# Attention of the second pair one step earlier, and both high casts ahead of the subtractions, in a fused attention and expert kernel

## The chip, the cores and the metric

The kernel runs on one core of a Trainium2 chip. The metric is the device time in microseconds (us) of one execution; three runs of the kernel before gave 1276.99, 1277.06 and 1277.22 us, median 1277.06. The profile is of one further execution.

## The reference

```python
def sm_attn(qq, kk, vv):                     # softmax(scale * qq kk^T) vv
    s = scale * np.matmul(qq, kk.transpose(0, 1, 3, 2))
    s = s - np.max(s, axis=-1, keepdims=True)
    a = np.exp(s)
    a = a / (np.sum(a, axis=-1, keepdims=True) + 1e-09)
    return np.matmul(a, vv)
p_packed = sm_attn(p, k, v)                  # 8 batches, 8 heads, 32 x 64
x = sm_attn(q, p_packed, p_packed)           # 8, 8, 576 x 64 -> 4608 x 512
for e in range(4):                           # p = domain_probs / its row sum
    h = np.maximum(x @ w1[e], 0.0)           # 512 x 1024
    out += p[:, e:e + 1] * (h @ w2[e])       # 1024 x 512
```

All is float32.

## The kernel before, in words

TensorE's share is written as 64 units. A unit is one batch `b` (576 tokens) and one chunk `ch` of 512 hidden columns (8 chunks: 4 experts, two halves each). Batches go in four pairs `sb`; within a pair the order is chunk by chunk, first the pair's even batch, then its odd one. Units are called u0 to u63 here, so from u3 on an even number is an even batch; u0 to u15 belong to the first pair, u16 to u31 to the second. The kernel's `step` is `2 * ch + b % 2`, which is the unit's number within its pair (only u1 and u2 are exchanged).

A unit does three things on TensorE, interleaved by hand. Seven products (`product`, index `i` from 0 to 6, 12 matmuls each, a scheme of seven products for a two by two block product) multiply this unit's hidden block with w2. Four groups (`mm1_groups`, 12 matmuls each) make the next unit's hidden block. And every even unit from u4 on forms the folded rows of the next chunk for both batches (`g_form`): packed values times w1, so that the second attention product and w1 become one matmul. `g_form` is a generator; the loop advances it after product 3 and after product 6, one row `g` each time, or in most units of the later pairs both rows in one advance (`rows = [range(NG)]`).

Every operand of the large matmuls is kept as a high and a low half. ScalarE casts the high half (`hi_of`, line 119), and the low half is a subtraction (`lo_of`, line 123), on VectorE for folded rows (`ghl`), on GpSimd for the products' operands (`st`), for the w2 operands (`tt`) and for the attention weights (`xl`). One PSUM tile `dbl` of two banks holds one row `g` of both batches, a bank each. There are four such tiles, which fill PSUM, so a matmul whose tile is still being read waits, and so does all of TensorE behind it.

Lines that the steps below touch: 71 and 81 (matmuls, by one helper or another), 76 (transposes), 391 (VectorE evicts a hidden block), 734 (VectorE sums of hidden blocks), 781 (sums of w2 blocks), 863 (VectorE adds a product to its sum), 896 (the seven sums combined after a batch's last chunk).

Attention of a later pair runs inside the units of the pair before it, as four generators: `pack_unit` for g = 0 and 1 (packed values of four heads each: load k, load v, scores, exponentials, transposes, product with v), then `tok_unit` for g = 0 and 1 (token weights: load q, scores, VectorE transposes into tile `a` at line 269, maximum at 274, exponentials on ScalarE at 279, sum at 289, division at 295, transpose at 304, high and low halves). For the first pair `AT_FIRST` names the steps at which each generator is made; at that moment what is left of the one before is drained. A generator is advanced once after every second product, and after every product from the third piece's step on. Each piece serves both batches of the pair.

The order of instructions on an engine is not the order of the text. A planner places them by their readiness in its own model of time, with the text's order as priority; only TensorE's groups and a few marked instructions are tied by hand. So on VectorE, ScalarE, GpSimd and on the queue of SyncE the order is fixed before the run, and an instruction that waits holds up all behind it on its engine. The program waits by tile.

Of the kernel before, what the change touches and what calls it, by code (L numbers as in the profile page):

```python
# [42 lines left out]
def attention_moe(ctx: ExitStack, tc: tile.TileContext, q, k, v, p, dp, w1, w2, out):  # L43
    nc = tc.nc
# [33 lines left out]
    def together(calls):  # L78

        for i, kw in enumerate(calls):  # L80
            ins = nc.tensor.matmul(**kw).ins  # L81
            for prev in order["free"] if i == 0 else []:
                after(ins, prev)
            if order["last"] is not None:
                after(ins, order["last"])
            order["last"] = ins
        order["free"] = []

    def dbl():
        return banks["dbl"].tile([P, 2, 512], F32, name="dbl")  # L90
# [21 lines left out]
    def cols(b, hh):  # L112

        i = (hh + b) % 2
        return slice(i * NPK, (i + 1) * NPK)

    def hi_of(dst, src, eng):
        if eng is nc.scalar:
            return nc.scalar.copy(out=dst, in_=src)  # L119
        return eng.tensor_copy(out=dst, in_=src)  # L120

    def lo_of(dst, src, hi, eng):
        return eng.tensor_tensor(out=dst, in0=src, in1=hi.bitcast(F32), op=ALU.subtract)  # L123
# [187 lines left out]
    def w1_load(ch, prs=range(NPAIR)):  # L311
        e, hf = divmod(ch, F // FC)
        res = []
        for pr in prs:
            raw = wpool.tile([P, FC], F32, name="wraw", bufs=4)
            load = nc.sync.dma_start(out=raw, in_=w1[e, pr * P:(pr + 1) * P, hf * FC:(hf + 1) * FC])
            res.append(raw)
        marks.setdefault(("w1", ch), load.ins)
        return res
# [3 lines left out]
    def g_tile(kept=False):  # L323
        if kept:
            return glast.tile([P, 2, FC], F32R, name="ghl6")
        return gpool.tile([P, 2, FC], F32R, name="ghl", bufs=5)

    def g_form(bs, ch, raws, rows=None, kept=None):

        for gr in rows or [[g] for g in range(NG)]:  # L330
            pss, calls = {}, []
            for g in gr:
                ps = dbl()
                pss.update({(b, g): ps[:, b % 2] for b in bs})
                for hs in range(4):
                    pr, hh = 2 * g + hs // 2, hs % 2
                    part = slice(hh * D, (hh + 1) * D)
                    for b in bs:
                        c0 = (hs // 2) * 2 * NPK + cols(b, hh).start
                        calls.append(dict(  # L340
                            out=pss[b, g][c0:c0 + NPK, :], lhsT=ppbd[b % 4][part, pr, cols(b, hh)],
                            rhs=raws[pr][part, :], start=True, stop=True,
                        ))
            together(calls)
            tiles = {(b, g): g_tile((b - bs[0], g) == kept) for b in bs for g in gr}
            for g in gr:
                for b in bs:
                    ghl = tiles[b, g]
                    hi_of(ghl[:, 0, :], pss[b, g], nc.scalar)
                    marks[b, ch, g, "low"] = lo_of(ghl[:, 1, :], pss[b, g], ghl[:, 0, :], nc.vector).ins  # L350
                    gs.setdefault((b, ch), []).append(ghl)
            yield
# [8 lines left out]
    def load_probs(b, e):  # L361
        t = wpool.tile([P, S], F32, name="pbt", bufs=2)
        nc.sync.dma_start(out=t, in_=pnd[e:e + 1, b * S:(b + 1) * S].partition_broadcast(P))
        pbt[b] = t
# [60 lines left out]
    def first_loads(pools):  # L425

        b = units[0][2]
        nfull = S // P
        r = S - nfull * P
        pt = small.tile([P, NPAIR, NPK], F32, name="pt")  # L430
        nc.sync.dma_start(out=pt, in_=p[b])
        kts, vts = [], []
        for g in range(NG):
            kts.append(pools[g].tile([P, 2, S], F32, name="kt"))
            nc.sync.dma_start(out=kts[g], in_=k[b][:, 2 * g:2 * g + 2, :])
        for g in range(NG):
            vt, vr = pools[g].tile([P, nfull, 4 * D], F32, name="vt"), pools[g].tile([P, 4 * D], F32, name="vr")
            nc.sync.dma_start(
                out=vt, in_=v[b, 0:nfull * P, g * 4 * D:(g + 1) * 4 * D].rearrange("(c p) d -> p c d", p=P),
            )  # L440
            nc.sync.dma_start(out=vr[0:r], in_=v[b, nfull * P:S, g * 4 * D:(g + 1) * 4 * D])
            vts.append([vt[:, c, :] for c in range(nfull)] + [vr])
        xs[b] = x_tiles(b)
        qts, raws = [], []
        for g in range(NG):
            qts.append(att_tile(b, [P, 2, S], "kt"))
            nc.sync.dma_start(out=qts[g], in_=q[b][:, 2 * g:2 * g + 2, :])
            raws += w1_load(0, range(2 * g, 2 * g + 2))
        return pt, kts, vts, qts, raws
# [473 lines left out]
    def drain(gen):  # L923
        for _ in gen:
            pass
# [6 lines left out]
    with ExitStack() as first:  # L932
# [9 lines left out]
        pt, kts, vts, qts, raws = first_loads(pools)  # L942
# [28 lines left out]
    GROUPS = {1: ((0, 0),), 3: ((0, 1),), 4: ((1, 1),), 6: ((1, 0),)}  # L971
    GROUPS_LAST = {1: ((0, 0),), 3: ((1, 0),), 4: ((0, 1),), 6: ((1, 1),)}
    GROUPS_LATE = {4: ((0, 0), (0, 1)), 5: ((1, 1),), 6: ((1, 0),)}
    AT_FIRST = ((4, pack_unit, 0), (7, pack_unit, 1), (9, tok_unit, 0), (12, tok_unit, 1))
    def second_tile(n):
        beside = {}

        def new(b, shape, name):
            if name == "kt" or name == "vt" and n == 1:
                return xpool.tile(shape, F32, name=("xh2", "xl2", "xh3", "xh2")[n] if name == "kt" else "xl3")  # L980
            if name == "vr":
                beside["at"] = att_tile(b, [P, 4 * D + len(SC) * P], "kt")
                return beside["at"][:, 0:4 * D]
            if name == "at" and n == 1:
                return beside["at"][:, 4 * D:].rearrange("p (c s) -> p c s", s=P)
            return att_tile(b, shape, name)
        return new
# [13 lines left out]
    for u, (sb, ch, b) in enumerate(units):  # L1001
# [4 lines left out]
        if sb + 1 < SB:  # L1006
            pair = [2 * sb + 2, 2 * sb + 3]
            for at_step, make, g in AT_FIRST if sb == 0 else AT_LATER:
                if at_step == step:
# [5 lines left out]
        if u == 2 or u == 3:  # L1015
            gsteps = g_form([1] if u == 2 else [0, 1], u - 1, raws)
            drain(gsteps)
            raws = w1_load(u)
        elif 3 < u <= AHEAD and not odd and nsb < SB:
            how = {}  # L1020
            if sb > 0:
                turn = ch if u < AHEAD else NCH - 2
                how["kept"] = (1, 0) if turn == 0 else (None, (0, 1), (1, 1))[(turn - 1) % 3]
                if turn > 0:
                    how["rows"] = [range(NG)]
            gsteps = g_form([2 * nsb, 2 * nsb + 1], nch, raws, **how)
# [20 lines left out]
        for i in range(NPROD):  # L1047
# [27 lines left out]
            if u == 1 and i == 3:  # L1075
                drain(second)
                drain(g_form([1], 0, raws))
                raws = w1_load(1)
            for _ in range(SECOND[u][i] if u in SECOND and i < len(SECOND[u]) else 0):
                next(second, None)  # L1080
            if i == 4 and u > 1 and u + 2 < len(units) and units[u + 2][1] % 2 == 0:
                load_probs(units[u + 2][2], units[u + 2][1] // 2)
            if i in (EVEN if odd or sb == 0 else AROUND) or sb == 0 and step >= AT_FIRST[2][0]:
                next(back, None)
# [16 lines left out]
        if u == 0:  # L1101
            raws = w1_load(0)
            load_probs(1, 0)
        elif not odd and u > 2:
            nsb, nch = (sb, ch + 2) if ch + 2 < NCH else (sb + 1, ch + 2 - NCH)
            if nsb < SB:
                raws = w1_load(nch)
# [34 lines left out]
```

## Time and profile before

| | |
|---|---|
| median of three runs | 1277.06 us |
| profiled execution | 1276.54 us |
| its span, first to last instruction | 1274.8 us |
| busy in the span: TensorE, VectorE, GpSimd, ScalarE | 1257.8, 962.5, 852.7, 494.4 us |
| TensorE's granted clock | 1.00 of full speed |

Engines are PE (TensorE), PEld (its weight loads), DVE (VectorE), ACT (ScalarE), POOL (GpSimd) and SP (SyncE, which issues nearly all DMAs). A line like "A <- B: t, n, m" in a view of waits says that A stood idle t us in all, n times, at most m us, until B had finished. Stretches of one unit are cut at the first matmul of the unit's first product, found by counting 84 product matmuls to a unit.

### The profile page before, as it was taken

To read this page: it belongs to the slowest core of one execution; us is meant where nothing else is said; L and a number is where in the kernel's file an instruction comes from. 1 tells how busy PE (TensorE), PEld (TensorE's weight loads), DVE (VectorE), ACT (ScalarE), POOL (GpSimd) and SP (SyncE) were. 2 spreads that over 40 slices of the span, in tenths; PEclk is the share of its full clock that TensorE was granted. 3 is DMA by queue.
4 is the path that set the end of the run, shared out by engine and by line. 5 is a ranking of instruction groups with operands and counts; after the bars stand their busy time and mean duration, and the time that the engine had idled before them with its cause. 6 is when DMAs were issued, how large, how long until landed. Compare 5 with 4: busy or idle time off the path is not lost.

```text
span 1274.8 us, 26918 instructions
## 1 busy us (share of the span) xinstructions
PE 1257.8 (99%) x10784; PEld 1172.9 (92%) x10784; DVE 962.5 (76%) x1315; ACT 494.4 (39%) x893; POOL 852.7 (67%) x564
## 2 busy tenths in 40 slices
PE   9999999999999999999999999999999999999998
PEld 6889998998999999999999999999999999999998
DVE  6866767899975767997786667799679567766776
ACT  4644545646344333333335423333323533333321
POOL 3779887898995545666578454476568755556575
PEclk9999999999999999999999999999999999999999
DMA  9995556635455554454454546433536443444562
GB/s 327 352 327 195 193 186 209 206 117 188 161 204 198 177 168 142 158 169 152 149 158 160 173 159 200 154 120 114 158 126 214 153 136 115 129 154 131 176 218 99
DMA packets 91708, 223.94 MB, mean 176 GB/s; under 512 B 9280, under 2 KB 32192, under 8 KB 91584
## 3 DMA queue, kind: packets, MB, share of 16 engines
q1 hardware_dynamic: 90768, 221.92, 52.6%
q8 instruction: 86, 1.41, 0.5%
q10 hardware_dynamic: 816, 0.30, 0.1%
q14 instruction: 38, 0.31, 0.1%
HBM read 183.31 MB, written 38.87 MB: 174 GB/s over the span
## 4 chain that ended last, share of the span: by engine, by line
PE 68%; POOL 15%; DVE 10%; issue 3%; ACT 2%; DMA 1%; SPq 0%; ACTq 0%; DVEq 0%; POOLq 0%
PE dbl L71 63%; POOL st L123 9%; PE dbl L81 4%; DVE sblk L734 3%; POOL tt L123 2%; POOL acc L896 2%; DVE ghl L123 1%; DVE acc L863 1%; DVE ablk L391 1%; POOL xl L123 1%; POOL b L781 1%; PE bank L81 1%; PE dbl L76 1%; ACT ghl L119 1%; ACT st L119 1%
## 5 line engine op out<-in xcount | busy, mean ns | idle before, releaser
L71 PE MATMUL dbl<-st,tt 128*128 128x288 f32 x5376 | 763.5, 296 | 6.3 <-POOL st L123 1.9
L71 PEld LDWEIGHTS dbl<-st,tt 128*128 128x128 f32 x5376 | 721.5, 188 | 50.4 <-issue 25.2
L123 POOL TENSOR_TENSOR st<-sblk,st 128x576 fp32r<-128x576 f32 x248 | 390.5, 1583 | 232.1 <-ACT st L119 219.6
L71 PE MATMUL dbl<-xh,ghl 128*128 128x288 f32 x2016 | 406.5, 294 | 2.2 <-DVE ghl L123 2.2
L123 POOL TENSOR_TENSOR st<-ablk,st 128x576 fp32r<-128x576 f32 x191 | 289.9, 1522 | 136.6 <-ACT st L119 130.0
L863 DVE TENSOR_TENSOR acc<-dbl,acc 128x576 f32<-128x576 f32 x385 | 287.7, 751 | 101.4 <-PE dbl L71 99.9
L71 PEld LDWEIGHTS dbl<-xh,ghl 128*128 128x128 f32 x2016 | 321.8, 188 | 2.9 <-DVE ghl L123 2.9
L391 DVE SCALAR_TENSOR_TENSOR ablk<-dbl,pbt 128x576 f32<-128x576 f32 x252 | 189.4, 752 | 140.9 <-PE dbl L71 140.2
L71 PE MATMUL dbl<-xl,ghl 128*128 128x288 f32 x1008 | 295.8, 294 | 0.0
L119 ACT CAST st<-sblk 128x576 fp32r<-128x576 f32 x252 | 170.7, 677 | 279.8 <-DVE sblk L734 221.2
L119 ACT CAST st<-ablk 128x576 fp32r<-128x576 f32 x193 | 130.6, 677 | 251.5 <-PE dbl L71 226.4
L71 PEld LDWEIGHTS dbl<-xl,ghl 128*128 128x128 f32 x1008 | 188.9, 188 | 0.3 <-POOL xl L123 0.3
L734 DVE TENSOR_TENSOR sblk<-ablk 128x576 f32<-128x576 f32 x126 | 136.5, 1084 | 9.2
L119 ACT CAST ghl<-dbl 128x512 fp32r<-128x512 f32 x124 | 70.7, 588 | 112.5 <-DVE ghl L123 58.1
L123 DVE TENSOR_TENSOR ghl<-dbl,ghl 128x512 fp32r<-128x512 f32 x124 | 83.4, 687 | 20.1 <-ACT ghl L119 18.0
L734 DVE TENSOR_TENSOR sblk<-ablk,sblk 128x576 f32<-128x576 f32 x63 | 78.0, 1238 | 5.4
L81 PE MATMUL dbl<-wraw,ppbd 64*32 64x512 f32 x992 | 64.5, 597 | 0.4 <-DVE acc L863 0.4
L123 POOL TENSOR_TENSOR tt<-b,tt 128x512 fp32r<-128x512 f32 x42 | 61.7, 1480 | 3.3 <-ACT tt L119 3.2
L734 DVE TENSOR_TENSOR sblk<-sblk,ablk 128x576 f32<-128x576 f32 x63 | 57.7, 915 | 1.2
L896 POOL TENSOR_TENSOR acc<-acc,acc 128x576 f32<-128x576 f32 x28 | 43.5, 1562 | 12.5 <-DVE acc L863 12.5
L861 ACT COPY acc<-dbl 128x576 f32<-128x576 f32 x55 | 35.3, 642 | 37.1 <-PE dbl L71 37.1
L896 DVE TENSOR_TENSOR acc<-acc,acc 128x576 f32<-128x576 f32 x28 | 33.3, 1195 | 0.6
(137 smaller groups left out, 475.9 us busy)
## 6 DMA issues: line engine op xcount, KB each, us to landing
tt<-td SPq DMA_DIRECT2D x192, 512.0 KB, 4.3
wraw<-in_w SPq DMA_DIRECT2D x136, 256.0 KB, 3.7
td<-tt SPq DMA_DIRECT2D x56, 512.0 KB, 3.7
pbt<-pnd SPq DMA_DIRECT2D x32, 288.0 KB, 4.1
out<-acc SPq DMA_DIRECT2D x31, 288.0 KB, 2.4
kt<-in_k SPq DMA_DIRECT2D x14, 576.0 KB, 6.2
kt<-in_q SPq DMA_DIRECT2D x14, 576.0 KB, 5.6
vt<-in_v SPq DMA_DIRECT2D x15, 512.0 KB, 5.7
```

The lines of the kernel that those rows point to most:

```text
L71: res = nc.tensor.matmul(**kw)
L76: on_pe(nc.tensor.transpose(**kw))
L81: ins = nc.tensor.matmul(**kw).ins
L119: return nc.scalar.copy(out=dst, in_=src)
L123: return eng.tensor_tensor(out=dst, in0=src, in1=hi.bitcast(F32), op=ALU.subtract)
L391: res = nc.vector.scalar_tensor_tensor(out=a, in0=ps[:, :, 0:HS], scalar=0.0, in1=probs.rearrange("p (o t) -> p o t", o=1).broadcast_to([P ...
L734: marks["sum", u, name] = nc.vector.tensor_tensor(out=t, in0=blk(x), in1=blk(y), op=op).ins
L781: op = eng[m].tensor_tensor(out=blk[place], in0=blk[x], in1=blk[y], op=ALU.subtract).ins
L861: marks["evicted"] = nc.scalar.copy(out=dst, in_=src).ins
L863: res = nc.vector.tensor_tensor(out=accs[b, i], in0=ps, in1=accs[b, i], op=ALU.add)
L896: eng.tensor_tensor(out=m[dst], in0=m[x], in1=m[y], op=op)
```

## The change

`g_form` gets a switch `apart`. With it, ScalarE's high casts of all tiles of one advance are written first, and then VectorE's subtractions; without it, cast and subtraction of a tile stand together, tile after tile. It is on in every even unit from u4 on that forms folded rows, but for u16 (`ch` is the chunk of the unit in which the rows are formed, so `ch > 0 or sb > 1` leaves out only the second pair's first unit). The four attention pieces for the second pair are made at steps 3, 6, 8 and 11 in place of 4, 7, 9 and 12. The rule that a generator is advanced after every product follows the third piece, so it holds from step 8 on.

```diff
-    def g_form(bs, ch, raws, rows=None, kept=None):
+    def g_form(bs, ch, raws, rows=None, kept=None, apart=False):
...
             tiles = {(b, g): g_tile((b - bs[0], g) == kept) for b in bs for g in gr}
+            for g in gr if apart else ():
+                for b in bs:
+                    hi_of(tiles[b, g][:, 0, :], pss[b, g], nc.scalar)
             for g in gr:
                 for b in bs:
                     ghl = tiles[b, g]
-                    hi_of(ghl[:, 0, :], pss[b, g], nc.scalar)
+                    if not apart:
+                        hi_of(ghl[:, 0, :], pss[b, g], nc.scalar)
                     marks[b, ch, g, "low"] = lo_of(ghl[:, 1, :], pss[b, g], ghl[:, 0, :], nc.vector).ins
...
-    AT_FIRST = ((4, pack_unit, 0), (7, pack_unit, 1), (9, tok_unit, 0), (12, tok_unit, 1))
+    AT_FIRST = ((3, pack_unit, 0), (6, pack_unit, 1), (8, tok_unit, 0), (11, tok_unit, 1))
...
         elif 3 < u <= AHEAD and not odd and nsb < SB:
             how = {}
+            how["apart"] = ch > 0 or sb > 1
```

## Rows read from the trace of the kernel before

**Rows 1.** The page: busy time, share of the span and instructions of each engine.
```profile
PE 1257.8 (99%) x10784; PEld 1172.9 (92%) x10784; DVE 962.5 (76%) x1315; ACT 494.4 (39%) x893; POOL 852.7 (67%) x564
```
**Rows 2.** Windows, three stretches: length, then busy us (count) of each engine.
```profile
102.98:362.44 259.46, 254.47 (x2228) 236.16 (x2221) 218.49 (x272) 125.94 (x281) 230.62 (x152) 1.00 0.54 188
362.44:672.18 309.74, 308.43 (x2682) 289.70 (x2681) 234.76 (x329) 111.12 (x183) 191.29 (x125) 1.00 0.50 162
1030.90:1067.73 36.83, 36.83 (x297) 35.28 (x297) 25.83 (x35) 11.63 (x18) 20.72 (x14) 1.00 0.43 137
```
**Rows 3.** Waits of TensorE, from u3 to the end of u8.
```profile
PE dbl L76 <- ACT ppn L233: 0.9, 2, 0.5
PE dbl L76 <- ACT a L198: 0.8, 1, 0.8
```
**Rows 4.** Waits of TensorE, from u9 to the end of u16.
```profile
PE dbl L71 <- DVE ghl L123: 1.8, 1, 1.8
PE dbl L71 <- POOL st L123: 0.6, 2, 0.4
PE dbl L71 <- DVE acc L863: 0.6, 1, 0.6
```
**Rows 5.** Waits of TensorE, from u17 to the end of u32.
```profile
PE dbl L71 <- DVE ghl L123: 0.9, 2, 0.5
```
**Rows 6.** Windows of u8 to u14: as Rows 2.
```profile
203.64:226.56 22.92, 22.48 (x255) 19.86 (x252) 14.77 (x20) 10.19 (x23) 16.16 (x12) 1.00 0.53 172
226.56:245.33 18.77, 18.77 (x165) 17.96 (x166) 16.38 (x25) 13.97 (x48) 15.11 (x11) 1.00 0.61 207
245.33:265.04 19.71, 19.71 (x167) 17.71 (x165) 19.54 (x25) 9.89 (x21) 19.71 (x13) 1.00 0.58 203
265.04:283.32 18.28, 17.71 (x140) 17.50 (x133) 16.26 (x19) 7.07 (x12) 17.56 (x13) 1.00 0.39 132
283.32:304.43 21.11, 21.11 (x198) 18.26 (x196) 19.75 (x28) 16.20 (x53) 17.55 (x13) 1.00 0.65 231
304.43:324.41 19.98, 18.06 (x140) 17.59 (x133) 18.80 (x22) 7.39 (x13) 19.38 (x13) 1.00 0.26 97
324.41:344.54 20.13, 19.78 (x166) 17.71 (x164) 19.83 (x23) 7.96 (x13) 20.13 (x13) 1.00 0.54 183
```
**Rows 7.** Windows of u9, u10, u12 and u13, instructions on tile a alone.
```profile
226.56:245.33 18.77, 0.00 (x0) 0.00 (x0) 3.81 (x7) 6.93 (x31) 0.00 (x0) 1.00 0.61 207
245.33:265.04 19.71, 0.00 (x0) 0.00 (x0) 5.09 (x5) 1.18 (x5) 0.00 (x0) 1.00 0.58 203
283.32:304.43 21.11, 0.00 (x0) 0.00 (x0) 5.21 (x9) 8.24 (x36) 0.00 (x0) 1.00 0.65 231
304.43:324.41 19.98, 0.00 (x0) 0.00 (x0) 3.33 (x3) 0.00 (x0) 0.00 (x0) 1.00 0.26 97
```
**Rows 8.** Timeline of u13's start, VectorE and ScalarE: start, duration, instruction, idle before.
```profile
308.11 1.83 DVE L295 TENSOR_TENSOR a<-a,s 128x576 f32<-128x576 f32 x1
309.86 0.68 DVE L123 TENSOR_TENSOR ghl<-dbl,ghl 128x512 fp32r<-128x512 f32 x1
...
310.57 0.59 ACT L119 CAST ghl<-dbl 128x512 fp32r<-128x512 f32 x1 [3.05 <-DVE ghl L123]
```
**Rows 9.** All instructions of line 295: duration ns least, median, most.
```profile
L295 DVE TENSOR_TENSOR a<-a,s x13: 760/1514/1990, 65.9 to 875.3; 128x576 f32<-128x576 f32 x13
```
**Rows 10.** Waits of all engines: ScalarE's high casts behind VectorE.
```profile
ACT ghl L119 <- DVE ghl L123: 58.1, 57, 3.2
```
**Rows 11.** Timeline in u24: casts, subtractions and the stall.
```profile
534.48 0.58 ACT L119 CAST ghl<-dbl 128x512 fp32r<-128x512 f32 x1
...
535.82 1.07 ACT L119 CAST ghl<-dbl 128x512 fp32r<-128x512 f32 x2 [0.76 <-DVE ghl L123]
...
536.44 1.29 DVE L123 TENSOR_TENSOR ghl<-dbl,ghl 128x512 fp32r<-128x512 f32 x2 [0.65 <-ACT ghl L119]
...
537.39 3.40 PE L71 MATMUL dbl<-st,tt 128*128 128x288 f32 x24 [0.46 <-DVE ghl L123]
```

## The prediction

> **What bounds the kernel now.** First the page's busy times, to see which engine fills the span: TensorE is busy 1257.8 of 1274.8 us [rows 1]. The granted clock is 1.00, so the matmuls can't run faster, and the change takes none away. What it can win is TensorE's idle time alone. Second, windows by stage show where that lies. Two units without attention take 36.83 us with no idle time; u3 to u15 have 259.46 - 254.47 = 4.99 us of it, u16 to u31 only 309.74 - 308.43 = 1.31 [rows 2]. (The end of a matmul is modelled, so a stall is some 0.1 to 0.2 us longer than its row; I leave that out.) Third, the waits of TensorE name who is late. From u3 to u8 it is the packing piece on ScalarE: 0.9 us for two transposes of the packed values and 0.8 for one after the exponentials [rows 3]. From u9 to u16 it is VectorE and GpSimd: 1.8 us for the low half of a folded row, 0.6 for a product's sum on VectorE (a PSUM tile not yet free), 0.6 for low halves of the products on GpSimd [rows 4]. From u17 on it is the folded rows again, 0.9 us in two stalls [rows 5], and the same answer comes for the next sixteen units.
>
> Why VectorE is late shows in the windows by unit: it is busy 19.54 of 19.71 us in u10, 19.75 of 21.11 in u12, 18.80 of 19.98 in u13, 19.83 of 20.13 in u14; u8 has 14.77 of 22.92 [rows 6]. The token pieces' work on VectorE is 3.81 + 5.09 = 8.90 us for the one in u9 and u10 and 5.21 + 3.33 = 8.54 for the one in u12 and u13 [rows 7]. The largest stall, at the start of u13, ends with a subtraction of a folded row that stood behind the token division, 1.83 us long [rows 8].
>
> **The change part by part.**
>
> *Packing pieces (steps 4 and 7 to 3 and 6).* Loads, scores, exponentials, casts and products are the same in number. What changes is the kind of unit: the first began in an even unit and now begins in an odd one, the second the other way round. The late exponentials belong to the odd start (u7), a transpose of packed values was late at the last advance of either piece [rows 3]. So I expect the same 0.9 + 0.8 us at other places: 0. Ends: the 0.8 goes, or comes twice, so -0.8 to +0.8. The loads of k and v go to SyncE's queue a unit earlier; a load takes effect by the tile that it waits for, and that tile comes free a unit earlier too. No wait of TensorE on a load stands in rows 3 to 5: 0.
>
> *Token pieces (steps 9 and 12 to 8 and 11).* Nothing is added; VectorE's 8.90 and 8.54 us move, and GpSimd's low halves with them. I take each piece's split by the kind of unit in which it starts: 5.21 + 3.33 from an even start, 3.81 + 5.09 from an odd one. Taken out of rows 6, VectorE without tokens needs 14.77 (u8), 16.38 - 3.81 = 12.57 (u9), 19.54 - 5.09 = 14.45 (u10), 16.26 (u11), 19.75 - 5.21 = 14.54 (u12), 18.80 - 3.33 = 15.47 (u13), 19.83 (u14). Put in again one unit earlier: u8 19.98 of 22.92, u9 15.90 of 18.77, u10 14.45 of 19.71, u11 20.07 of 18.28, u12 19.63 of 21.11, u13 15.47 of 19.98. So u8 takes 5.21 us where there was room for 8.15, and u13 and u14, which follow one another with no room, get 3.33 us back. The sore place becomes u11: 1.79 us over. Part of its 16.26 is work left from u10, whose own excess goes, and the scores' matmuls lengthen u11 too, so I expect a stall of about the size of today's at u11, 0.6, and 0.4 for GpSimd's share. Of 1.8 + 0.6 + 0.6 = 3.0 us [rows 4], 1.0 stay: -2.0. Ends: all 3.0 go; or u11's excess adds 1.8 to what is there. Between them I am nearer to the first, because the excess is worked out for one unit and the room in u8, u9 and u10 together is 2.94 + 2.87 + 5.26 = 11.1 us.
>
> *High casts first.* A folded row's tile holds both batches, and the second batch's cast waits today until the first batch's subtraction has ended: ScalarE stands idle 58.1 us in 57 such waits [rows 10]. None of that is TensorE's time except where the row is late. In u24 the order is cast at 534.48, subtraction, casts from 535.82, subtractions from 536.44 to 537.73, and a product waits until 537.39 for the row's PSUM tile [rows 11]. Now both casts of the row end by about 534.48 + 1.07 = 535.55. The subtraction then waits for the second cast, as today the cast waits for the subtraction. Two subtractions take 1.29 us [rows 11] and end at 536.84. The first row's second one ends today 0.64 after 536.44, at 537.08: 0.24 earlier. Four such stalls, two in each of the two answers of 0.9 [rows 5], give -1.0. Ends: all four go, -1.8; or four new ones of that size appear where VectorE now waits for the second cast with sums and evictions behind it, +1.8. Some twenty further advances of the later pairs have no stall (rows 5 names all), so each has slack today, and a wait of one cast is 0.58 [rows 11]; that is why I stay near the row.
>
> In the first pair the same edit ends ScalarE's wait of 3.05 us at 310.57 [rows 8], behind which casts for the products stood. That helps GpSimd's lateness, and I count it in the 2.0.
>
> What the row doesn't show is whether the subtraction has to wait for the second cast at all. The Trainium skill, "PSUM — Partial Sum Buffer", section "Specifications (TRN2)", says that ScalarE and VectorE can read PSUM in parallel as long as no bank collides; the two batches lie in different banks. By that rule the first subtraction could run beside the second cast. Rows 10 and 11 speak against it for this program, which waits by tile; by the rule the part would be -1.8 and not -1.0.
>
> Sum: 0 - 2.0 - 1.0 = -3.0 us. The profiled execution took 1276.54 us (span 1274.8 and 1.7 around it), so 1273.5 by its own time; it lies 0.5 below the median of the runs, and from the median 1277.06 - 3.0 = **1274.1 us**.
>
> **Rivals.**
>
> *The stall only moves.* VectorE's work is the same in sum, and u3 to u15 use 218.49 of 259.46 us of it [rows 2]; what was late at u11 and u13 is then late at u9 and u12. For it: u12's even start was followed by the worst stall, and the even start is now u8's. Against it: u8 has room. Then only the casts pay: 1277.06 - 1.0 = 1276.1.
>
> *Slower: the division in front of the folded rows, twice.* Line 295 takes 0.76 us at best and 1.99 at worst [rows 9], at the tail of each token piece. If the planner puts it in front of the subtraction at u9 as it did at u13, the 1.8 comes there. At u11 the 1.79 over delays the rows for u12, and since u12 is then full (19.63 + 1.79 = 21.42 of 21.11) the delay lasts into u13, another 1.8. With today's 0.6 of GpSimd that is 6.0 for 3.0; if the casts give nothing the time is 1280.1. It decides itself at u11: with less than about 1 us over, u12 catches up. Speaking for this case is the Trainium skill, "SBUF — State Buffer", section "SBUF: two separate sides": VectorE with two SBUF inputs and GpSimd exclude one another for a whole instruction. Row 9's spread agrees with it, and GpSimd is busy 17.56 of 18.28 us in u11 [rows 6].
>
> *Nothing holds the subtraction back.* By bank, the four late stalls go and the sum is -3.8: 1273.3. The skill's PSUM rule, above, would have it so; rows 10 and 11 don't.
>
> *The casts' order doesn't change much.* The planner decides by its own times, and ScalarE's order may come out as before, since it doesn't see the stall. Then 1277.06 - 2.0 = 1275.1.
>
> **How the numbers follow.** A measurement of this kernel can tell 0.2% from no change, 2.55 us: faster means below 1274.5, slower above 1279.6. My forecast has 0.42: 0.36 of it below 1274.5, since its terms add up to anything from -4.6 to -1.5, and 0.06 within. The stall that moves has 0.29 (0.27 within, 0.02 slower). The division twice has 0.12, all of it slower. No hold by bank has 0.09, all faster. The order unchanged has 0.08 (0.06 within, 0.02 faster). Faster 0.47, same 0.39, slower 0.14. The range reaches down to 1271.5 (all of rows 4 and most of the late stalls) and up to 1278.5; the forecast alone has 1272.5 to 1275.6.
>
> **What would show it.** Right: windows of u8 with VectorE near 20 us and of u13 well under 18; no wait of 1.8 us on a folded row at u13; two casts of a row back to back on ScalarE and its waits behind VectorE nearly gone; the four late stalls at 0.2 each. Wrong: a wait on a folded row at u9 or u12 as long as the old one, or u14 and u15 as full as before, or stalls on the transposes of the packing pieces that add up to more than 1.7. The prediction fails as a whole if TensorE's idle time from u3 to u15 stays at 5.

## The result, and the profile after

The change makes the kernel slower by 0.7%: 1286.99 us, the median of four runs (1284.06 to 1287.93), against 1277.03 (1276.92 to 1277.22, four runs). The ratio is 1.0072, with a 95% interval of 1.0059 to 1.0084. Forecast was 1274.1, in a range of 1271.5 to 1278.5.

The profiled execution after took 1287.34 us, 10.8 more than the 1276.54 of before. The page first, with the busy times.

```profile
PE 1261.1 (98%) x10784; PEld 1176.6 (92%) x10784; DVE 949.6 (74%) x1315; ACT 491.3 (38%) x893; POOL 851.0 (66%) x564
```

The instructions are as many as in [rows 1], but TensorE is busy 3.3 us longer with them. The windows of u3 to u15 and of u16 to u31 (length, busy us and count of each engine, granted clock, DMA share, GB/s) say where the time went:

```profile
103.88:374.82 270.94, 258.79 (x2229) 239.91 (x2221) 221.89 (x273) 126.05 (x282) 229.84 (x152) 0.98 0.53 181
374.82:682.76 307.94, 307.57 (x2682) 289.61 (x2681) 229.22 (x328) 109.43 (x181) 188.82 (x125) 1.00 0.50 162
```

Against [rows 2], u3 to u15 take 270.94 - 259.46 = 11.5 us more. TensorE's idle time there went from 4.99 to 270.94 - 258.79 = 12.15, which is 7.2 of it; the other 4.3 is matmul time, at a mean clock of 0.98. From u16 to u31 the change wins 1.8 us, and over the next sixteen units 0.6 (308.87 for 309.46). The stages ahead of u3 and behind u47 add 0.9 and 0.8. Ahead of u3 no engine's order is changed, and that stage takes 102.87 to 103.88 us over all the kernels of this document, so its 0.9 is scatter. (Of the 2.4 us won in the later pairs, 0.9 + 0.3 is idle time in the rows; the rest is shorter matmul time, which no row here explains.)

TensorE's waits from u3 to u15 name who was late ("A <- B: total us, times, longest"):

```profile
PE dbl L71 <- POOL st L123: 4.7, 3, 2.7
PE dbl L76 <- ACT ppn L233: 3.9, 1, 3.9
PE dbl L76 <- ACT a L198: 1.8, 1, 1.8
...
PE dbl L71 <- DVE ghl L123: 0.7, 2, 0.4
```

VectorE's 1.8 us on a folded row [rows 4] is gone. In its place GpSimd's low halves are late by 4.7 instead of 0.6, and ScalarE in the packing pieces by 3.9 + 1.8 instead of the 0.9 + 0.8 of [rows 3]. Each of the three large stalls has a place in the timeline (start, duration, instruction, idle before and what ended it). The largest is in u7, in the second packing piece:

```profile
207.97 0.48 SPq L772 DMA_DIRECT2D b<-in_w  x1
...
208.17 0.32 PE L71 MATMUL dbl<-vr,at 64*32 64x64 f32 x8
...
211.47 0.62 ACT L119 CAST tt<-b 128x512 fp32r<-128x512 f32 x1 [4.10 <-DMA b<-in_w]
...
212.00 0.31 ACT L233 ACTIVATE ppn<-dbl,rs 128x64 f32<-128x64 f32 x1
...
212.36 0.42 PE L76 MATMUL dbl<-ident,ppn 128*64 128x128 f32 x1 [3.88 <-ACT ppn L233]
```

The product with v has ended by about 208.5. The scaling of its result (line 233) takes 0.31 us, but stands on ScalarE behind the cast of a w2 block for a later unit, and that cast waits 4.10 us at the head of the queue for a load issued only at 207.97. TensorE waits 3.88 for the scaling. In u3 the same happens on a smaller scale: a w2 cast that waits for a sum on GpSimd (line 785) stands ahead of the copies of the scores.

```profile
120.42 0.62 ACT L119 CAST tt<-b 128x512 fp32r<-128x512 f32 x1 [3.55 <-POOL b L785]
120.95 1.18 ACT L190 COPY a<-dbl 128x576 f32<-128x576 f32 x2
...
125.31 0.77 PE L76 MATMUL dbl<-ident,a 128*128 128x128 f32 x5 [1.83 <-ACT a L198]
```

In u14 three low halves of w2 operands run on GpSimd in front of the low half of a product's operand that TensorE needs:

```profile
336.61 4.29 POOL L123 TENSOR_TENSOR tt<-b,tt 128x512 fp32r<-128x512 f32 x3
...
340.85 1.40 POOL L123 TENSOR_TENSOR st<-sblk,st 128x576 fp32r<-128x576 f32 x1
...
342.30 2.41 PE L71 MATMUL dbl<-st,tt 128*128 128x288 f32 x12 [2.67 <-POOL st L123]
```

The windows of u8 and of u12 to u14, which answer to [rows 6]:

```profile
212.46:235.65 23.19, 23.19 (x197) 20.39 (x198) 15.97 (x26) 14.45 (x51) 11.13 (x8) 0.90 0.51 178
...
294.65:315.66 21.01, 19.77 (x166) 17.69 (x164) 20.30 (x25) 10.15 (x19) 21.01 (x14) 1.00 0.48 166
315.66:333.14 17.48, 17.48 (x140) 17.48 (x133) 14.89 (x15) 6.02 (x10) 17.48 (x13) 1.00 0.33 120
333.14:357.34 24.20, 21.53 (x167) 19.29 (x165) 19.84 (x24) 8.61 (x14) 20.23 (x14) 0.93 0.45 155
```

VectorE has the room in u13 that was forecast, 14.89 of 17.48. GpSimd (the last of the busy columns) has none in u12 and u13: 21.01 of 21.01 and 17.48 of 17.48; before, it had 3.56 us of room in u12 (17.55 of 21.11) and 0.60 in u13 [rows 6].

The casts did what was said. ScalarE's waits behind the subtractions, 58.1 us before [rows 10], in the view of all engines:

```profile
ACT ghl L119 <- DVE ghl L123: 3.9, 4, 1.4
```

And u24, against [rows 11], has four casts back to back; the subtraction starts at 546.76, when the second cast ends, and the stall is 0.18 where it was 0.46; the profile puts what is left down to TensorE's own matmuls and no longer to the row. The second fence is TensorE's waits from u17 into u48: the four stalls have 0.8 us together, where each of the two answers of [rows 5] had 0.9 for two (0.6 us in two stalls behind GpSimd is new there).

```profile
545.66 2.05 ACT L119 CAST ghl<-dbl 128x512 fp32r<-128x512 f32 x4
...
546.76 2.48 DVE L123 TENSOR_TENSOR ghl<-dbl,ghl 128x512 fp32r<-128x512 f32 x4 [0.52 <-ACT ghl L119]
...
548.31 1.95 PE L71 MATMUL dbl<-st,tt 128*128 128x288 f32 x13 [0.18 <-PE dbl L71]
```

```profile
PE dbl L71 <- PE dbl L71: 0.8, 4, 0.2
```

### The profile page after: what moved, and what is told of

Same layout as the page of the kernel before. It is cut to its first block, busy times and chain, and to the rows that moved or that the text cites. A ratio compares the mean times of both kernels' runs of the same rounds, so it can differ in the third digit from the quotient of the medians.

```text
span 1285.5 us, 26979 instructions
## 1 busy us (share of the span) xinstructions
PE 1261.1 (98%) x10784; PEld 1176.6 (92%) x10784; DVE 949.6 (74%) x1315; ACT 491.3 (38%) x893; POOL 851.0 (66%) x564
## 4 chain that ended last, share of the span: by engine, by line
PE 77%; POOL 12%; DVE 4%; issue 3%; ACT 2%; DMA 1%; SPq 0%; POOLq 0%; ACTq 0%; DVEq 0%
PE dbl L71 71%; POOL st L123 6%; PE dbl L81 5%; POOL tt L123 3%; POOL b L785 1%; DVE sblk L738 1%; PE bank L81 1%; PE dbl L76 1%; POOL acc L900 1%; ACT a L279 1%; DMA b<-in_w 1%; ACT st L119 0%; POOL xl L123 0%; DMA kt<-in_k 0%; ACT tt L119 0%
## 5 line engine op out<-in xcount | busy, mean ns | idle before, releaser
L738 DVE TENSOR_TENSOR sblk<-ablk 128x576 f32<-128x576 f32 x126 | 125.7, 998 | 9.6 <-POOL st L123 0.5
L123 DVE TENSOR_TENSOR ghl<-dbl,ghl 128x512 fp32r<-128x512 f32 x124 | 78.2, 682 | 14.4 <-ACT ghl L119 14.0
L119 ACT CAST ghl<-dbl 128x512 fp32r<-128x512 f32 x124 | 65.1, 595 | 56.5 <-PE dbl L81 52.6
L738 DVE TENSOR_TENSOR sblk<-ablk,sblk 128x576 f32<-128x576 f32 x63 | 70.3, 1115 | 6.6 <-POOL st L123 1.2
L119 ACT CAST tt<-b 128x512 fp32r<-128x512 f32 x42 | 24.9, 619 | 35.0 <-DMA b<-in_w 14.1
```

The costliest lines, as they stand in the source:

```text
L738: marks["sum", u, name] = nc.vector.tensor_tensor(out=t, in0=blk(x), in1=blk(y), op=op).ins
```

## The experiments

Ratios are to the kernel before, with their 95% intervals; medians are over all runs of a kernel. The kernel before was run again beside each group of kernels, with medians of 1276.87, 1277.02 and 1277.0 us, and a ratio need not be the quotient of two medians. The theory: the early packing pieces put waiting w2 casts ahead of their own ScalarE work. The rivals: the casts' order or the token pieces cost the time.

**The two halves of the change.** First the casts alone:

```diff
-    AT_FIRST = ((3, pack_unit, 0), (6, pack_unit, 1), (8, tok_unit, 0), (11, tok_unit, 1))
+    AT_FIRST = ((4, pack_unit, 0), (7, pack_unit, 1), (9, tok_unit, 0), (12, tok_unit, 1))
```

> Casts ahead of the subtractions, attention steps as before (4, 7, 9, 12). Theory A (the slowdown comes from the packing pieces' earlier start: at u7 ScalarE's cast of a w2 block that still waits for its load stands ahead of the scaling of the packed values): no stall above 1 us before u9, TensorE's clock 1.00 throughout, the later pairs as in the changed kernel, about 1.2 us less than before; 1275 to 1276.5 us. Rival B (the casts' new order upset ScalarE's queue): 1284 or more, with the u7 stall.

Measured 1278.0 (1275.5 to 1283.88, 11 runs), ratio 1.0001 [0.9989, 1.0014]. TensorE's waits from u3 to u15:

```profile
PE dbl L71 <- DVE ghl L123: 3.0, 3, 2.1
PE dbl L76 <- ACT ppn L233: 1.1, 2, 0.6
PE dbl L76 <- ACT a L198: 1.1, 1, 1.1
```

The 3.9 us of u7 isn't there, which leaves rival B out, and the folded row's stall at u13 is 2.1 in place of 1.8. The later pairs win 0.9 and 0.7 us, and u3 to u15 lose 2.3 (261.76). So theory A has the place right and the time not: the median lies above its 1276.5, the clock does fall behind the stall of u13, and 1.1 us stand before u9. Then the steps alone:

```diff
-            how["apart"] = ch > 0 or sb > 1
+            how["apart"] = False
```

> Steps 3, 6, 8, 11, casts as before. Theory A: the u7 stall of some 3.9 us and the dip of the clock stand here too; 1286 to 1290 us, and the later pairs have the old 0.4 us stalls. Rival B: about 1277.

Measured 1288.73 (1287.53 to 1289.08, 4 runs), ratio 1.0088 [1.0074, 1.0102]. Of TensorE's waits from u3 to u15:

```profile
PE dbl L76 <- ACT ppn L233: 3.6, 1, 3.6
PE dbl L71 <- DVE ghl L123: 3.4, 3, 1.8
PE dbl L76 <- ACT a L198: 1.8, 1, 1.8
```

The folded rows' 3.4 us are new against the changed kernel's 0.7. The longest is in u9, behind a token division:

```profile
239.25 1.83 DVE L295 TENSOR_TENSOR a<-a,s 128x576 f32<-128x576 f32 x1
...
241.73 0.40 PE L71 MATMUL dbl<-xh,ghl 128*128 128x288 f32 x1 [1.83 <-DVE ghl L123]
```

That is the stall, the place and the length that the prediction's slower rival gave for u9. With the casts first it doesn't come: in the changed kernel the division stands in front of the subtractions there too (from 237.70, for 1.99 us), and no stall on a folded row is over 0.4.

The steps alone cost the whole loss. The casts' order gives back some 1.7 us (1288.73 - 1286.99), though the two intervals overlap.

**Which pieces.** The packing pieces early, the token pieces at their old steps, casts first:

```diff
-    AT_FIRST = ((3, pack_unit, 0), (6, pack_unit, 1), (8, tok_unit, 0), (11, tok_unit, 1))
+    AT_FIRST = ((3, pack_unit, 0), (6, pack_unit, 1), (9, tok_unit, 0), (12, tok_unit, 1))
```

> Packing pieces at 3 and 6 as in the changed kernel, token pieces at 9 and 12 as before, casts ahead. Theory A: the stalls at u3 (1.8 us) and u7 (about 3.9 us, then the clock at half) stand here; 1281 us or more. Rival C (the token pieces' move, VectorE and GpSimd behind at u11 to u14, costs most): under 1279.

Measured 1283.32 (1282.87 to 1287.38, 4 runs), ratio 1.0054 [1.004, 1.0068]: three quarters of the loss (1.0054 of 1.0072), as theory A said. The stalls of u7 and u3 are both there (and, with the token pieces at their old steps, the 2.1 us of the casts alone at u13):

```profile
PE dbl L76 <- ACT ppn L233: 3.2, 1, 3.2
...
PE dbl L76 <- ACT a L198: 1.8, 1, 1.8
```

The last token piece alone early, casts first:

```diff
-    AT_FIRST = ((3, pack_unit, 0), (6, pack_unit, 1), (8, tok_unit, 0), (11, tok_unit, 1))
+    AT_FIRST = ((4, pack_unit, 0), (7, pack_unit, 1), (9, tok_unit, 0), (11, tok_unit, 1))
```

> Casts ahead and only the last token piece early: steps 4, 7, 9, 11. Theory as predicted before the run (moving token work out of u13 and u14 helps VectorE): u13's 2.1 us stall goes, 1274 to 1276. Rival: GpSimd takes the place of VectorE; stalls of 1 us or more on its low halves at u12 and u14, 1278 to 1282.

Measured 1278.88 (1277.91 to 1279.31, 10 runs), ratio 1.001 [1.0001, 1.0019]. The stall on the folded row at u13 is gone, and the one on GpSimd is there, with two w2 low halves ahead:

```profile
329.88 3.05 POOL L123 TENSOR_TENSOR tt<-b,tt 128x512 fp32r<-128x512 f32 x2
...
334.34 1.85 PE L71 MATMUL dbl<-st,tt 128*128 128x288 f32 x12 [2.69 <-POOL st L123]
```

So this step trades 2.1 us behind VectorE for 2.7 behind GpSimd, as the rival said. The first token piece wasn't moved by itself.

**The order on one engine, and nothing else.** The changed kernel with one tie added, which puts the w2 cast behind the scaling in u7; ScalarE's order alone differs:

```diff
-                nc.scalar.mul(ppn, ps[:, 0, 0:D], rss[b])
+                marks["ppn", b, g] = nc.scalar.mul(ppn, ps[:, 0, 0:D], rss[b]).ins
...
+            if ch == 5 and i == 0:
+                after(high.ins, marks["ppn", 3, 1])
```

> The changed kernel with one order more: the first cast of the w2 block that u9 forms may not come before the scaling of the packed values of the second piece's last batch. Only ScalarE's order changes. Theory A: no 3.9 us stall at u7 and no dip there, at least 6 us less than the changed kernel, 1281 or below; and if the stall at u14 is work on GpSimd that the u7 stall had pushed back, that one shrinks too, down to 1277. Rival C: the u7 stall goes but the time comes back at the next late operand, 1284 or more.

Measured 1281.01 (1280.45 to 1282.09, 6 runs), ratio 1.0032 [1.002, 1.0043], which is 6.0 us less than the changed kernel by the medians and 5.1 by the ratios. The timeline in u7:

```profile
207.92 0.31 ACT L233 ACTIVATE ppn<-dbl,rs 128x64 f32<-128x64 f32 x1 [0.29 <-PE dbl L71]
...
208.28 0.30 PE L76 MATMUL dbl<-ident,ppn 128*64 128x128 f32 x1 [0.43 <-ACT ppn L233]
...
211.80 0.62 ACT L119 CAST tt<-b 128x512 fp32r<-128x512 f32 x1 [3.58 <-DMA b<-in_w]
```

The cast still waits 3.58 us for the load, and nobody waits for it. In the two traces u7 and u8 together take 41.79 us in place of 47.31. That settles u7. The stall at u14 isn't work that the u7 stall had pushed back: it stays, at 2.69. The same for u3, on top of it (ScalarE's order; a few neighbours on other engines shift by one place):

```diff
+                marks["copied", b, g] = nc.scalar.copy(out=a1v, in_=raw).ins
...
+            if ch == 2 and i == 4:
+                after(high.ins, marks["copied", 3, 0])
```

> f1 with one order more on ScalarE: the cast of the w2 block that waits for GpSimd's sum in u3 comes behind the two copies of the first packing piece's scores. Theory A (both packing stalls are a queue order on ScalarE): the 1.8 us stall at u3 shrinks to under 0.6, about 1.4 us less than f1, 1279.5. Rival: the exponentials are late anyway (VectorE's maximum), the stall stays above 1.2 and the time within 0.5 us of f1.

Measured 1279.24 (1278.4 to 1279.99, 10 runs), ratio 1.0012 [1.0003, 1.0021], 1.8 us less by the medians and 2.6 by the ratios (the intervals of the two kernels just overlap); the stall of 1.83 is 0.44:

```profile
123.11 0.76 PE L76 MATMUL dbl<-ident,a 128*128 128x128 f32 x5 [0.44 <-ACT a L198]
```

And u14, again on top of the first tie: w2 low halves behind the products' operands, GpSimd's order alone.

```diff
-            lo_of(t[:, 1], blk[n], t[:, 0], nc.gpsimd)
+            low = lo_of(t[:, 1], blk[n], t[:, 0], nc.gpsimd)
+            if ch == NCH - 1 and i > 3:
+                after(low.ins, marks[False, "operand"])
```

> f1 with one order more on GpSimd: in u14 the last low halves of the w2 block come behind the product operands' low halves already made. Theory: the 2.7 us stall at u14 and the clock's dip after it are this order on a GpSimd that has no idle time left, so they shrink to about 1 us and none, 3 to 4 us less than f1, 1277 to 1278. Rival (GpSimd is simply behind by that much): the stall moves to the w2 operand, the time within 1 us of f1.

Measured 1278.62 (1278.02 to 1279.88, 10 runs), ratio 1.0008 [0.9999, 1.0017], 2.4 us less (3.1 by the ratios), short of the theory's 3 to 4 by the medians; the stall of 2.69 is 0.25:

```profile
333.20 1.96 POOL L123 TENSOR_TENSOR st<-sblk,st 128x576 fp32r<-128x576 f32 x1
...
335.22 1.85 PE L71 MATMUL dbl<-st,tt 128*128 128x288 f32 x12 [0.25 <-POOL st L123]
```

**All three ties in the changed kernel:**

```diff
+            if ch == NCH - 1 and i > 3:
+                after(low.ins, marks[False, "operand"])
...
+            if ch == 5 and i == 0:
+                after(high.ins, marks["ppn", 3, 1])
+            if ch == 2 and i == 4:
+                after(high.ins, marks["copied", 3, 0])
```

> The changed kernel with the three order ties of f1, f2 and f3 together. Theory A with the GpSimd order: each tie gives what it gave alone, 6.0 + 1.8 + 2.4 = 10.2 us off the changed kernel's 1287.0, so 1276.5 to 1277.5, the time before; the early steps then cost and gain about nothing. Rival: the waits share their slack, and 1278.5 or more remains.

Measured 1277.28 (1276.83 to 1278.27, 10 runs), ratio 1.0002 [0.9993, 1.0011]. The single effects give 1286.99 - 6.0 - 1.8 - 2.4 = 1276.8; by the ratios they add up to 10.7 us, and the three ties together take off 8.9, so each price is good to a microsecond or two. So three orders on two queues account for the loss, and the change with them mended is worth nothing that can be measured. By the profiles, u16 to u31 and u32 to u47 keep the casts' gain (308.80 and 308.77 us, 0.9 and 0.7 less than before), and it is spent elsewhere: u3 to u15 take 260.39, 0.9 more than before, the stage behind u47 0.8 more, and the stage ahead of u3, scatter again, 0.7 more. In u3 to u15 GpSimd remains the latest:

```profile
PE dbl L71 <- POOL st L123: 2.4, 4, 1.2
```

**A better version?** The casts alone, and the token division behind the folded row at u13:

```diff
+            if (b, g) == (3, 1):
+                after(marks[b, g, "mul"], marks[1, NCH - 1, 1, "low"])
```

> Casts ahead, old steps, and one order more on VectorE: the last token piece's division (line 295) comes behind the subtractions of the folded rows formed in u12. Theory: the 2.1 us stall at u13 falls to about 0.3 and with it the dip of the clock that follows it in some runs; 1273 to 1275, faster than both kernels. Rival: the stall was work, not order; it moves to the token weights or to a product, 1275 to 1278.

Measured 1276.48 (1276.09 to 1277.27, 11 runs), ratio 0.9993 [0.9984, 1.0002].

```profile
309.58 1.28 DVE L123 TENSOR_TENSOR ghl<-dbl,ghl 128x512 fp32r<-128x512 f32 x2
...
310.31 0.40 PE L71 MATMUL dbl<-xh,ghl 128*128 128x288 f32 x1 [0.39 <-DVE ghl L123]
...
310.78 2.02 DVE L295 TENSOR_TENSOR a<-a,s 128x576 f32<-128x576 f32 x1
```

The stall at u13 is 0.39 in place of the 2.1 of the casts alone; but 1.2 us behind GpSimd and 0.8 behind VectorE's sums appear in u13 and u14, as the rival said. With GpSimd's tie as well, and the casts together with the subtractions again in u32 and u48 (`ch > 0` leaves out the first unit of every pair):

```diff
+            if ch == NCH - 1 and i > 3:
+                after(low.ins, marks[False, "operand"])
...
-            how["apart"] = ch > 0 or sb > 1
+            how["apart"] = ch > 0
```

> g1 with GpSimd's order of f3 as well (and the casts together again in u32 and u48). Theory: the 1.2 us stall of g1 at u14 shrinks to about 0.4; 1275.3 to 1276, about 0.1% under the kernel before. Rival: the low halves of the w2 block become late instead, no better than g1's 1276.5.

Measured 1276.6 (1276.09 to 1277.85, 11 runs), ratio 0.9997 [0.9988, 1.0006]. That is no better than without the tie, and neither can be told from the kernel before. Their spans are shorter, 1274.3 us (median of either kernel's 11 runs) against 1275.2. But in each of these runs 2.2 to 2.3 us of the time lie outside the span, against 1.7 to 1.9 in the kernel before; the casts alone and the last token piece alone have 2.2 to 2.3 too, all other kernels 1.7 to 1.9. Why, no run here shows.

## Why the prediction was wrong

**The packing pieces: the step that failed.** "So I expect the same 0.9 + 0.8 us at other places: 0", with ends of -0.8 and +0.8. The two orders on ScalarE cost 6.0 and 1.8 us by the medians, 5.1 and 2.6 by the ratios. The mistake is in the bounds: they count the piece's own transposes and take ScalarE's work ahead of them as unchanged. Even the upper ends of all three parts, 0.8 + 1.8 + 1.8 = 4.4, would have given only 1281.5; and its own sign of being wrong came, stalls on these transposes of 3.9 + 1.8 = 5.7 us where 1.7 was the limit. What stands ahead in an in-order queue is the planner's choice, and it was made anew. The trace of before had the sign of it, in the waits of all its engines:

```profile
ACT tt L119 <- DVE b L781: 10.6, 6, 3.8
ACT tt L119 <- DMA b<-in_w: 7.3, 4, 2.3
```

ScalarE's w2 casts wait there at the head of its queue, up to 3.8 us for VectorE and 2.3 for a load, and TensorE's waits show nothing behind them. Any of these could come to stand ahead of a packing piece; 3.8 us would have been an upper end for each of the two places; the stalls were 3.88 and 1.83, and the clock's price comes on top of the first.

**The loads: 0.** "No wait of TensorE on a load stands in rows 3 to 5" is true, and proved nothing: a load, of w2 and not of k or v, held TensorE through ScalarE. That chain has two links, and the row shows the last one alone.

**The token pieces: -2.0, half right.** VectorE's lateness went as forecast: u13 is under 18, and no wait of 1.8 stands there. The pieces' work on tile `a` moved as worked out: 5.79 us in u8, 2.91 in u9, 3.97 in u11 and 5.52 in u12, for 5.21, 3.33, 3.81 and 5.09. But u8 did not come near 20 (15.97): beside the piece it has 15.97 - 5.79 = 10.18 us of other work, where 14.77 was taken from before; which work left the unit no row here names. u11 has 19.79 of 20.25, near the 20.07 worked out, and TensorE 0.8 idle there. The term that failed is GpSimd's, whose low halves move with the piece: it was put at 0.4 and measured 4.7, and the upper end of the part adds nothing for it. Its 19.38 of 19.98 us in u13 [rows 6] was a warning that I read only for VectorE. And VectorE's part holds only together with the casts: with the steps alone, 1.83 us stand behind a division in u9. The stall at u14, 2.7 us, stays with the last piece alone moved, and goes with GpSimd's order alone: 2.4 us.

**The casts: -1.0, right in mechanism and near in size.** The four late stalls fell from 1.8 us together to 0.8; the later pairs won 2.4 us in all in the changed kernel and 1.6 with the casts alone. The first subtraction waits for the second cast, as [rows 10, 11] had it: between the two banks of one tile the reads are in order. Between the tiles of the two rows they are not. In u24 the last two of the four casts run until 547.71, beside the subtractions that began at 546.76, so for 0.95 us both engines read PSUM. The Trainium skill, "PSUM — Partial Sum Buffer", section "Specifications (TRN2)", says that ScalarE and VectorE can read PSUM in parallel as long as no bank collides. Between tiles the trace agrees; within a tile the order of the two reads leaves nothing to see of it. What the step missed is the first pair, where the casts alone leave the stall at u13 longer, 2.1 for 1.8, with a fall of the clock behind it in the profiled run.

**The rivals.** The slower one had the sign, but its 1280.1 and its place are not the changed kernel's, where no stall on a folded row is over 0.4 us; its stall at u9 came with the steps alone. The twelve divisions of line 295 in [rows 9] that are slow (1.06 to 1.99 us) ran beside GpSimd instructions from start to end, the one of 0.76 beside none. The range, up to 1278.5, left that rival's own time out; its lower end, 1271.5, doesn't follow from the terms that it names, since all of [rows 4] and all the late stalls are 3.0 + 1.8 = 4.8, which gives 1272.3. "The stall only moves" named the right kind of thing for the wrong engine: it moved to GpSimd, and grew. None had ScalarE's queue, and none a price for TensorE's clock, which the last section works out at some 4 us.

## What to carry to other kernels

A step that is moved in a planned program changes the order of all queues near it, so its bounds are not the moved work's own waits: take, for each engine that the critical engine waits for, the longest wait in the old trace that may come to stand ahead. Look in the waits of all engines for instructions that wait long at the head of an in-order queue for data that nobody needs soon; here one cast of 0.62 us, put in front with a wait of 4.10, cost 5 to 6. When such an order is found, tie those two instructions alone: that shows the cause, and mends it.

## What the runs showed of the hardware

A stall of TensorE can cost more than its length, because the granted clock may fall to half behind it. The changed kernel after u7's 3.88 us, in windows of 2 us (as above; the granted clock is the third number from the end):

```profile
212.00:214.00 2.00, 1.64 (x7) 1.64 (x8) 0.00 (x0) 0.72 (x4) 2.00 (x2) 0.50 0.98 300
214.00:216.00 2.00, 2.00 (x11) 2.00 (x10) 0.28 (x1) 0.23 (x1) 0.50 (x1) 0.50 1.06 394
216.00:218.00 2.00, 2.00 (x13) 2.00 (x13) 0.50 (x2) 0.46 (x2) 1.43 (x1) 0.74 0.98 377
```

0.50 is 1.2 GHz of 2.4; from 218 to 220 the clock is 1.00 again. Lost in busy time: 1.64 x 0.50 + 2 x 0.50 + 2 x 0.26 = 2.3 us, beside the 3.5 that the stall itself is longer than with the tie; together 5.8 of the 6.0 that the tie gave back. Behind u14's stall the clock falls as well (0.83, 0.50 and 0.81 in the three windows from 342 to 348, with 1.70, 2.00 and 2.00 us of matmuls), which costs 0.29 + 1.00 + 0.38 = 1.7 more: 4.0 of the 4.3 us of longer matmul time.

A stall of the same length doesn't always do it. u14's stall is 2.69 us both in the kernel with the first tie and in the one with the last token piece alone; the windows from 1.9 and 1.7 us behind its end, first the former, then the latter, with 10 matmuls in 2 us and 22:

```profile
338.00:340.00 2.00, 2.00 (x10) 2.00 (x9) 1.63 (x2) 0.67 (x1) 2.00 (x2) 0.50 0.50 181
```

```profile
336.00:338.00 2.00, 2.00 (x22) 1.72 (x28) 1.74 (x2) 0.67 (x1) 2.00 (x2) 1.00 0.63 221
```

What decides between them no run here shows. The price alone can be had from the first tie's kernel and the one with GpSimd's tie, which agree in order on all engines up to u6; in this stretch from u3 into u6 the clock falls behind the 1.8 us stall of u3 in the second alone:

```profile
103.30:172.36 69.06, 66.14 (x609) 62.06 (x601) 51.47 (x65) 31.84 (x63) 56.36 (x40) 1.00 0.53 183
```

```profile
103.21:173.85 70.64, 67.72 (x609) 63.62 (x601) 51.43 (x65) 31.85 (x63) 56.42 (x40) 0.98 0.51 179
124.70:128.10 3.40, 3.40 (x16) 3.36 (x17) 0.92 (x3) 2.06 (x7) 3.40 (x3) 0.50 0.76 289
```

TensorE is idle for 2.92 us in either, so all of 70.64 - 69.06 = 1.58 us is the price of these 3.40 at half. The Trainium skill, "TensorE: Matmul & The Clock Gate", section "Terms", puts the penalty at the throttled time times the share of pulses left out; as an estimate that is 1.7 here, and the rows agree. The spread of the casts alone goes with the clock: five of its runs have a mean clock of 1.000 and take 1275.5 to 1276.32 us; the other six have 0.993 to 0.999 and take 1278.0 to 1283.88. That isn't shown to be its cause, and doesn't hold for every kernel: of the runs of the kernel before, one with a mean clock of 0.998 took 1276.72 us, and one with 1.000 took 1278.62.
